# Attention tail: the last 64 queries of both heads of a pair handled as one tile of 128 rows

## The chip, the cores and the metric

The kernel runs on one core of a Trainium2 chip. The metric is the device time of one execution in microseconds. Before the change three runs gave 1061.9, 1064.76 and 1065.36 us, a median of 1064.76 us. The execution that the profiler took is a run of its own.

Engines are named as in the profile: PE is TensorE (PEld is its weight load), DVE is VectorE, ACT is ScalarE, POOL is GpSimd, and SP issues the DMAs.

## What is computed

The reference is three layers, one after the other. Only the first is touched:

```python
B, H, S, D = 2, 8, 576, 64
scores = matmul(q, k.T) / sqrt(D)                # per head, 576 x 576
scores = where(key > query, -1e9, scores)        # causal
a = exp(scores - max); a /= a.sum(-1) + 1e-9
local = a @ v
q_p = where(q > 0, q, exp(q) - 1) + 1
mem = (q_p @ M_prev) / (q_p . z_prev + 1e-6)
x = g * mem + (1 - g) * local                    # g = sigmoid(beta), per head
```

Its output, 1152 tokens by 512, goes through a softplus layer (512 to 2048 to 512) and then through a layer of 8 experts (512 to 1024 to 512 each) whose shares come from 8 rounds of row and column normalization.

## The kernel before, in words

Everything is one launch. The order of all instructions is worked out before by a planner (`Plan`): each operation is added with an engine, an assumed duration, the buffers that it reads and writes and a rank; `Plan.run` then starts, on each engine, the operation of lowest rank that is ready and whose buffers are free, and emits the instructions in the order of these planned starts. On the chip every engine works through its list in that order, and waits where an input is late. Durations are assumed by the small helpers `act`, `dve`, `gps`, `pe`, `dma`; `gps` is for GpSimd. An operation marked as using the shared port is not planned beside another such operation.

Attention runs over 8 units (2 batches, 4 pairs of heads), and in each unit over 5 query tiles, `QT`: four of 128 queries and a tail of 64 (queries 512 to 575). `prep` loads keys and queries of one head (transposed, doubled over the two halves of the partitions) and splits them into rounded parts and remainders in `st` (keys, queries, remainder of queries); `prep_v` loads values, a column of ones, and the queries for the memory branch, whose `phi` it works out.

`softmax(u, i)` computes the scores of one tile for both heads (lines 517 and 518: two products per head and part), adds the mask and takes the row minimum of the scaled negative on DVE (525), exponentiates on ACT (540), transposes the result in blocks of 128 keys on PE (548, 550) into the one PSUM bank `tp`, and copies it to SBUF as `pt` (270, the copy helper). The tail has 576 keys, more than one bank of PSUM holds, so its scores come in two parts of 288, and its rows are 64: one 64-row tile for each head, each with two score parts, one exponential, five transposes and two copies.

`output(u, i, pts)` multiplies `phi` with the memory (568), each head's `pt` with its values, in blocks of 128 keys and 65 columns (575), adds the small constants to the divisors (590), inverts them (592), scales (593), adds memory and local parts on GpSimd (275, the pair helper), transposes both heads at once (596), and `piece` copies the result and its remainder into the inputs of the next layer (270, 610). The output of a tile is ranked two tiles behind its softmax (`AHEAD`). A floating-point product that isn't rounded shows in the trace as two instructions, a transpose as one.

PSUM in attention: two banks `sp` for scores, one `tp`, two `pm`, one `xp`, and two more (`bank`) that scores may use in the first four units. From the fifth unit on the latter go to products of the next layer (676 to 678), which PE runs between those of attention as soon as batch 0 is done.

Of the kernel before, what the change touches and what calls it, by code (L numbers as in the profile page):

```python
# [19 lines left out]
P = 128  # L20
# [34 lines left out]
NPR, NPT = 6, 4  # L55
PS = (2, 1, 2, 1)
QT = [(0, 128), (128, 128), (256, 128), (384, 128), (512, 64)]

# [183 lines left out]
def fused_kernel(ctx, tc, kq, vq, gm, w_in, w_out, wg, w1, w2, out1, out2):  # L242
# [19 lines left out]
    def gps(n, fn, r, w, x=0, **kw):  # L262
        return pl.add("POOL", 90 + 2.23 * n + x, fn, r, w, port=True, **kw)
# [119 lines left out]
    def attention():  # L383
# [12 lines left out]
        mask = pl.buf("ac", [P, 512 + P], F32, "mask")  # L396
        eps = pl.buf("ac", [P, NPAIR, 4], F32, "eps")

# [7 lines left out]
        def consts():  # L406
            def masks():
                nc.gpsimd.memset(mask.ap, 0.0)
                nc.gpsimd.affine_select(
                    out=mask[:, 512:], in_=mask[:, 512:], compare_op=ALU.is_ge, fill=NEG,  # L410
                    base=0, pattern=[[-1, P]], channel_multiplier=1,
                )
                nc.gpsimd.memset(eps[:, :, 0:2], 1e-9)
                nc.gpsimd.memset(eps[:, :, 2:4], 1e-6)

            pl.add("POOL", 2000, masks, [], [mask, eps])

# [34 lines left out]
        def stack(u, j):  # L452
            st = pl.buf("ld", [P, 3, S], F32R, "st", "st")
            U[u]["qs", j] = st
            return st


        def prep(u, j):
            b, p = units[u]
            st = stack(u, j)  # L460
            kqd = pl.buf("ld", [P, 2, S], F32, "kqd", "kqd")
            low = "POOL" if u else "DVE"

            def part(lo, hi):
                n, c, k = hi - lo, slice(lo, hi), ("c", lo)
# [12 lines left out]
        def prep_v(u):  # L478
            b, p = units[u]
            vt = pl.buf("a2", [P, 5 * 130 + S], F32, "vt", "vt")  # L480
            ph = pl.buf("a2", [P, S], F32, "phi", "phi")
            dma(614, lambda: nc.sync.dma_start(vt.ap, vq[b, p]), [vt], late=2000)

            act(S, lambda: nc.scalar.activation(ph.ap, vt[:, 650:], AF.Exp), [vt], [ph])
            dve(S, lambda: nc.vector.tensor_scalar(
                out=ph.ap, in0=ph.ap, scalar1=1.0, scalar2=None, op0=ALU.min), [], [ph], fast=True)
            dve(S, lambda: nc.vector.scalar_tensor_tensor(
# [10 lines left out]
        def softmax(u, i):  # L498
# [3 lines left out]
            if kx <= 512:  # L502
                parts = [(0, max(kx, 256), kx)]
            else:
                parts = [(0, kx // 2, kx // 2), (kx // 2, kx // 2, kx // 2)]
# [5 lines left out]
            def part(k, k0, n, w):  # L511
# [3 lines left out]
                def mm():  # L515
                    for sp, st in zip(sps, sts):
                        nc.tensor.matmul(sp[:R, :n], st[:, 1, q0:kx], st[:, 0, k0:k0 + n], start=True, stop=False)  # L517
                        nc.tensor.matmul(sp[:R, :n], st[:, 2, q0:kx], st[:, 0, k0:k0 + n], start=False, stop=True)  # L518
# [3 lines left out]
                m0 = 512 - q0 + k0  # L522
# [13 lines left out]
            nb = (kx + P - 1) // P  # L536
            nf = min(nb, 4)

            def head(pr, mn):
# [3 lines left out]
                pt = pl.buf("a3", [P, 4 * P + 64], F32, "pt", "pt")  # L543
                tp = pl.buf("psa", [P, 512], F32, "tp", "tp")

                def tr():
                    for t in range(nf):
                        nc.tensor.transpose(tp[:, t * R:(t + 1) * R], pr[:R, t * P:(t + 1) * P], ident[:R, :R])  # L548
                    if nb == 5:
                        nc.tensor.transpose(tp[:64, 4 * R:5 * R], pr[:R, 512:576], ident[:R, :R])  # L550
# [3 lines left out]
                if nb == 5:  # L554
                    copy(R, lambda: pt[:64, 4 * R:5 * R], lambda: tp[:64, 4 * R:5 * R], [tp], [(pt, ("p", 1))],
                         psum=True)
# [3 lines left out]

        def output(u, i, pts):
            b, p = units[u]
# [8 lines left out]
            def pv(j):  # L571
# [7 lines left out]
                pe(nb * (223 if R == P else 119), mm, [pts[j], (vt, ("v", j))], [pm])  # L579
# [66 lines left out]
        return [gms, mask, eps] + [b for (p, t), q in pl.queues.items() if p in apools or p == "psa" for b in q]  # L646
# [798 lines left out]
def _layout(q, k, v, M_prev, z_prev, beta, moe_w_in, moe_w_out, moe2_w_gate, moe2_w1, moe2_w2):  # L1445
# [11 lines left out]
    kq = np.stack([k.transpose(0, 1, 3, 2), q.transpose(0, 1, 3, 2)], 3)  # L1457
# [5 lines left out]
    vq = np.concatenate([vp, q.transpose(0, 1, 3, 2).reshape(B, NPAIR, P, S)], 3)  # L1463
# [31 lines left out]
```

## Time and profile before

| | us |
|---|---|
| median of 3 runs | 1064.76 |
| the profiled execution | 1059.33 |
| its span, first to last instruction | 1057.6 |
| PE busy | 1041.1 (98%) |
| DVE busy | 922.8 (87%) |
| ACT busy | 593.2 (56%) |
| POOL busy | 364.2 (34%) |

Busy time of PE is of matmuls that overlap, with modelled ends. So the time that a group of them takes is read from its start to the start of the next group, not from its busy time. An attention unit is about 20 us of the first 160; the two other layers take the rest.

### The profile page before, as it was taken

Reading aid. Unit: us, or ns where it says so; the run is one execution under the profiler, and the core shown is the slowest. Engines: PE = TensorE matmul, PEld = TensorE weight load, DVE = VectorE, ACT = ScalarE, POOL = GpSimd, SP = SyncE. Lnnn points to the kernel's source line nnn. Section 1 sums busy time; section 2 is a strip of 40 time slices with the busy share of each in tenths; the row PEclk is TensorE's granted clock in tenths of the full one; section 3 lists DMA queues with packets and bytes.
Section 4 is the critical chain, followed back from the end, with each engine's and each line's share of the span. In section 5 each row is a group of like instructions: output and inputs, shape, how many; then the busy total and the mean of one; then the engine's idle time right before and its main releaser. Section 6 shows DMA issues by size and latency. Waiting matters only on the chain.

```text
span 1057.6 us, 14920 instructions
## 1 busy us (share of the span) xinstructions
PE 1041.1 (98%) x5262; PEld 869.7 (82%) x5262; DVE 922.8 (87%) x1738; ACT 593.2 (56%) x1144; POOL 364.2 (34%) x394
## 2 busy tenths in 40 slices
PE   6999999999999999999999999999999999999998
PEld 5888888788887878888888888888888888888886
DVE  6777779787868699999999999999999999999977
ACT  5787675656374766355554555545555455554542
POOL 3565535131342332434234233332333323233220
PEclk9999899999999999999999999999999999999999
DMA  5543111333320111211211111110121111111002
GB/s 203 172 141 112 64 62 40 100 100 100 99 81 21 60 41 48 84 41 59 76 45 60 53 48 60 60 60 29 53 79 42 60 45 56 56 54 59 22 20 90
DMA packets 28558, 72.89 MB, mean 69 GB/s; under 512 B 2684, under 2 KB 11972, under 8 KB 28484
## 3 DMA queue, kind: packets, MB, share of 16 engines
q1 hardware_dynamic: 28484, 71.95, 21.1%
q8 instruction: 41, 0.67, 0.3%
q14 instruction: 33, 0.27, 0.1%
HBM read 69.54 MB, written 2.40 MB: 68 GB/s over the span
## 4 chain that ended last, share of the span: by engine, by line
PE 93%; DVE 4%; ACT 1%; issue 1%; DMA 0%; POOL 0%; SPq 0%; DVEq 0%; ACTq 0%; POOLq 0%
PE pa L1185 6%; PE dA L1359 6%; PE pa L1186 6%; PE dA L1361 6%; PE pa L1187 6%; PE dA L1360 5%; PE pm L575 4%; PE pc L1185 3%; PE pc L1187 3%; PE pc L1186 3%; PE dC L1361 3%; PE dC L1360 3%; PE dC L1359 3%; PE tp L548 2%; PE dn L828 2%; PE dn L826 2%
## 5 line engine op out<-in xcount | busy, mean ns | idle before, releaser
L275 POOL TENSOR_TENSOR ws<-raw 128x256 f32<-128x256 f32 x128 | 124.7, 975 | 440.7 <-issue 20.4
L270 ACT ACTIVATE fh<-u 128x512 fp32r<-128x512 f32 x160 | 99.9, 627 | 100.8 <-DVE u L1285 51.8
L276 DVE TENSOR_TENSOR fl<-u,fh 128x512 fp32r<-128x512 f32 x160 | 115.7, 724 | 7.3 <-ACT fh L270 7.3
L1236 ACT ACTIVATE u<-pa 128x512 f32<-128x512 f32 x64 | 38.0, 594 | 64.8 <-PE pa L1187 64.1
L1376 DVE TENSOR_TENSOR acc<-dA,acc 128x512 f32<-128x512 f32 x92 | 61.7, 683 | 5.5 <-PE dA L1361 5.3
L270 ACT ACTIVATE fh<-t 128x512 fp32r<-128x512 f32 x64 | 38.6, 623 | 41.4 <-DVE t L1285 41.4
L575 PE MATMUL pm<-vt,pt 128*128 128x65 f32 (+2 forms) x480 | 58.5, 260 | 0.0
L575 PEld LDWEIGHTS pm<-vt,pt 128*128 128x128 f32 (+2 forms) x480 | 53.2, 177 | 4.5 <-issue 1.4
L275 POOL TENSOR_TENSOR ws<-raw,ws 128x256 f32<-128x256 f32 x64 | 55.1, 861 | 0.0
L275 POOL TENSOR_TENSOR ws<-ws,raw 128x256 f32<-128x256 f32 x64 | 53.0, 829 | 4.9
L270 ACT ACTIVATE pt<-tp 128x256 f32<-128x256 f32 (+3 forms) x96 | 35.4, 386 | 26.3 <-PE tp L548 17.5
L540 ACT ACTIVATE pr<-pr,mn 128x128 f32<-128x128 f32 (+4 forms) x80 | 45.6, 599 | 6.3 <-DVE mn L525 5.9
L1240 DVE TENSOR_TENSOR u<-pc,u 128x512 f32<-128x512 f32 x64 | 43.7, 683 | 3.5 <-PE pc L1187 1.8
L1256 ACT ACTIVATE pb<-pa 128x512 f32<-128x512 f32 x32 | 18.6, 582 | 48.9 <-PE pa L1187 44.8
L525 DVE CUSTOM_DVE_ANT_0 pr<-sp,mask 128x128 f32<-128x128 f32 (+4 forms) x80 | 36.3, 473 | 9.6 <-PE sp L518 4.5
L276 DVE TENSOR_TENSOR fl<-t,fh 128x512 fp32r<-128x512 f32 x64 | 44.1, 689 | 0.0
L275 POOL TENSOR_TENSOR st<-kqd,st 64x576 fp32r<-64x576 f32 (+1 forms) x28 | 40.3, 1444 | 8.0 <-DVE st L271 3.2
L1249 DVE SCALAR_TENSOR_TENSOR u<-u,pb 128x512 f32<-128x512 f32 x56 | 41.8, 746 | 0.6
L1376 DVE TENSOR_TENSOR acc<-dC,acc 128x512 f32<-128x512 f32 x62 | 40.9, 681 | 0.1
L517 PE MATMUL sp<-st 128*128 128x256 f32 (+3 forms) x96 | 34.8, 374 | 5.5 <-DVE st L276 5.5
L548 PE MATMUL tp<-ident,pr 128*128 128x128 f32 (+1 forms) x224 | 37.6, 273 | 2.7 <-ACT pt L270 2.1
L275 POOL TENSOR_TENSOR gl<-u,gh 128x512 fp32r<-128x512 f32 x12 | 15.5, 1296 | 62.0 <-ACT u L753 61.5
(5121 smaller groups left out, 3607.5 us busy)
## 6 DMA issues: line engine op xcount, KB each, us to landing
raw<-w SPq DMA_DIRECT2D x64, 512.0 KB, 3.5
raw<-w_in SPq DMA_DIRECT2D x16, 512.0 KB, 3.5
raw<-w_out SPq DMA_DIRECT2D x16, 512.0 KB, 3.5
kqd<-kq SPq DMA_DIRECT2D x14, 576.0 KB, 3.7
vt<-vq SPq DMA_DIRECT2D x8, 613.0 KB, 5.3
pb<-gates SPq DMA_DIRECT2D x16, 256.0 KB, 5.3
out<-acc SPq DMA_DIRECT2D x9, 256.0 KB, 2.0
kqd<-kq SPq DMA_DIRECT2D x2, 320.0 KB, 4.3
```

Of the source, the lines that this page charges most:

```text
L270: return act(n, lambda: nc.scalar.activation(out(), src(), AF.Copy), r, w, x=-42 if psum else 0, **kw)
L275: return gps(n, lambda: nc.gpsimd.tensor_tensor(out=out(), in0=a(), in1=b(), op=op), r, w, **kw)
L276: return dve(n, lambda: nc.vector.tensor_tensor(out=out(), in0=a(), in1=b(), op=op), r, w, port=True, **kw)
L548: nc.tensor.transpose(tp[:, t * R:(t + 1) * R], pr[:R, t * P:(t + 1) * P], ident[:R, :R])
L575: nc.tensor.matmul(pm[:R, j * 65:(j + 1) * 65], pts[j][:kk, t * R:(t + 1) * R], vt[:kk, t * 130 + j * 65:t * 130 + (j + 1) * 65], start=(t ...
L1185: nc.tensor.matmul(o[:, :CH], wh[:, at], h(), start=start and k == 0, stop=False, **kw)
L1186: nc.tensor.matmul(o[:, :CH], wh[:, at], l(), start=False, stop=False, **kw)
L1187: nc.tensor.matmul(o[:, :CH], wl[:, at], h(), start=False, stop=(k == 1), **kw)
L1359: nc.tensor.matmul(o[:, :CH], wh[:, at], h.ap, start=start and n == 0, stop=False, **kw)
L1360: nc.tensor.matmul(o[:, :CH], wh[:, at], l.ap, start=False, stop=False, **kw)
L1361: nc.tensor.matmul(o[:, :CH], wl[:, at], h.ap, start=False, stop=(n == 1), **kw)
L1376: dve(CH, lambda: nc.vector.tensor_tensor(out=acc[c][:, cs_], in0=o[:, :CH], in1=acc[c][:, cs_], op=ALU.add), [o], [a_])
```

## The change

The query columns of each head are laid out on the host with 128 columns in the tail, in which head 0 fills the first 64 and head 1 the last 64, and the rest is zero. The queries of the memory branch get a second copy of their last 64 columns. So the products of both heads can be accumulated into one score tile of 128 rows. The tail has one softmax (`both`) and one output (`output2`) for both heads. Rows 0 to 63 of the product with the values are used from the columns of head 0, rows 64 to 127 from those of head 1; the scaled rows are written into the two diagonal blocks of a tile `z`, zero elsewhere, and a product of `z` with two stacked identities (`fold`) replaces the transpose. Masks and these constants are made by more GpSimd operations at the start. `pr` has 5 buffers in place of 6. GpSimd's assumed duration in the planner goes from 90 + 2.23 n to 160 + 2.2 n ns.

```diff
-NPR, NPT = 6, 4
+NPR, NPT = 5, 4
 PS = (2, 1, 2, 1)
 QT = [(0, 128), (128, 128), (256, 128), (384, 128), (512, 64)]
+SQ = S + D
+TAIL = len(QT) - 1
...
-        return pl.add("POOL", 90 + 2.23 * n + x, fn, r, w, port=True, **kw)
+        return pl.add("POOL", 160 + 2.2 * n + x, fn, r, w, port=True, **kw)
...
-        mask = pl.buf("ac", [P, 512 + P], F32, "mask")
+        mask = pl.buf("ac", [P, 512], F32, "mask")
         eps = pl.buf("ac", [P, NPAIR, 4], F32, "eps")
+        mask2 = pl.buf("ac", [P, S // 2], F32, "mask2")
+        fold = pl.buf("ac", [P, D], F32, "fold")
+        z = pl.buf("ac", [P, P], F32, "z")
...
+            def tails():
+                nc.gpsimd.memset(mask2.ap, 0.0)
+                for j in range(2):
+                    r = slice(j * D, (j + 1) * D)
+                    nc.gpsimd.affine_select(
+                        out=mask2[r, :], in_=mask2[r, :], compare_op=ALU.is_ge, fill=NEG,
+                        base=512 - S // 2, pattern=[[-1, S // 2]], channel_multiplier=1,
+                    )
+                    nc.gpsimd.tensor_copy(fold[r, :], ident[r, r])
+                nc.gpsimd.memset(z.ap, 0.0)
...
-                dma(n, lambda: nc.sync.dma_start(kqd[:, :, c], kq[b, 2 * p + j, :, :, c]), [(kqd, k)],
-                    late=2500 if lo or u else 0)
-                kd, w = [(kqd, k)], [(st, k)]
-                copy(n, lambda: st[:, 0, c], lambda: kqd[:, 0, c], kd, w, eng="DVE")
-                copy(n, lambda: st[:, 1, c], lambda: kqd[:, 1, c], kd, w)
-                pair(n, lambda: st[D:, 0, c], lambda: kqd[D:, 0, c], lambda: st[D:, 0, c].bitcast(F32),
+                qhi = SQ if hi == S else hi
+                n, m, k = hi - lo, qhi - lo, ("c", lo)
+                kc, qc = slice(lo, hi), slice(S + lo, S + qhi)
+                lc = slice(S + SQ + lo, S + SQ + qhi)
+                src, late = kq[b, 2 * p + j], 2500 if lo or u else 0
+                if n == S:
+                    dma(608, lambda: nc.sync.dma_start(kqd.ap, src), [kqd], late=late)
+                elif not lo:
+                    def two(x):
+                        return x[:, :2 * S].rearrange("p (a c) -> p a c", a=2)[:, :, :hi]
+                    dma(n, lambda: nc.sync.dma_start(two(kqd), two(src)), [(kqd, ("c", 0, 0))], late=late)
+                else:
+                    for r, c in enumerate((kc, qc)):
+                        dma((c.stop - c.start) // 2, lambda c=c: nc.sync.dma_start(kqd[:, c], src[:, c]),
+                            [(kqd, ("c", lo, r))], late=late)
+                kd, w = [(kqd, ("c", lo, r)) for r in range(2 if lo else 1)], [(st, k)]
+                if n == S:
+                    kd = [kqd]
+                copy(n, lambda: st[:, kc], lambda: kqd[:, kc], kd, w, eng="DVE")
+                copy(m, lambda: st[:, qc], lambda: kqd[:, qc], kd, w)
+                pair(n, lambda: st[D:, kc], lambda: kqd[D:, kc], lambda: st[D:, kc].bitcast(F32),
                      ALU.subtract, kd, w, eng=low)
-                pair(n, lambda: st[:, 2, c], lambda: kqd[:, 1, c], lambda: st[:, 1, c].bitcast(F32),
+                pair(m, lambda: st[:, lc], lambda: kqd[:, qc], lambda: st[:, qc].bitcast(F32),
                      ALU.subtract, kd, w, eng=low)
...
+            dma(646, lambda: nc.sync.dma_start(vt.ap, vq[b, p]), [vt], late=2000)
...
+            if i == TAIL:
+                return both(u, sts)
+            parts = [(0, max(kx, 256), kx)]
...
-                pe(nb * (R / 1.2 + (3 if R == P else 9)), tr, [pr], [tp])
-                copy(nf * R, lambda: pt[:, :nf * R], lambda: tp[:, :nf * R], [tp], [(pt, ("p", 0))], psum=True)
-                if nb == 5:
-                    copy(R, lambda: pt[:64, 4 * R:5 * R], lambda: tp[:64, 4 * R:5 * R], [tp], [(pt, ("p", 1))],
-                         psum=True)
...
+        def both(u, sts):
+            w = S // 2
+            pr = pl.buf("a3", [P, S], F32, "pr", "pr")
+            mn = pl.buf("sm", [P, 2], F32, "mn", "mn")
+            def part(k):
+                k0 = k * w
+                sp = bank("sp") if not k and u < NPAIR else pl.buf("psa", [P, 512], F32, "sp", "sp")
+                def mm():
+                    for n, st in enumerate(sts):
+                        for m in range(2):
+                            q = S + m * SQ + 512
+                            nc.tensor.matmul(sp[:, :w], st[:, q:q + P], st[:, k0:k0 + w],
+                                             start=(n + m == 0), stop=(n + m == 2))
+                pe(4 * mms(w) + 30, mm, sts, [sp])
+                dve(w, lambda: nc.vector.tensor_tensor_reduce(
+                    out=pr[:, k0:k0 + w], in0=sp[:, :w], in1=mask2.ap if k else mask[:, :w], op0=ALU.add, op1=ALU.min, scale=-0.125,
+                    scalar=mn[:, 0:1] if k else 3.0e38, accum_out=mn[:, k:k + 1]),
+                    [sp, mask if not k else mask2], [pr, mn])
+                return sp
+            part(0)
+            sp = part(1)
+            act(S, lambda: nc.scalar.activation(pr.ap, pr.ap, AF.Exp, bias=mn[:, 1:2], scale=-1.0), [mn], [pr], x=93)
+            pt = pl.buf("a3", [P, 5 * P], F32, "pt", "pt")
+            tp = pl.buf("psa", [P, 512], F32, "tp", "tp")
+            def tr():
+                for t in range(4):
+                    nc.tensor.transpose(tp[:, t * P:(t + 1) * P], pr[:, t * P:(t + 1) * P], ident)
+            pe(4 * 110, tr, [pr], [tp])
+            pe(110, lambda: nc.tensor.transpose(sp[:D, 384:512], pr[:, 512:S], ident), [pr], [sp])
+            copy(512, lambda: pt[:, :512], lambda: tp.ap, [tp], [(pt, ("p", 0))], psum=True)
+            copy(P, lambda: pt[:D, 512:], lambda: sp[:D, 384:512], [sp], [(pt, ("p", 1))], psum=True)
+            return pt
+        def output2(u, pt):
+            b, p = units[u]
+            vt, ph = U[u]["v"], U[u]["phi"]
+            pm = pl.buf("psa", [P, 512], F32, "pm", "pm")
+            pe(220, lambda: nc.tensor.matmul(pm[:, 130:260], ph[:, 512:SQ], mds(u), start=True, stop=True),
+               [ph, (gms, ("g", b))], [pm])
+            def mm():
+                for t in range(5):
+                    kk = min(P, S - t * P)
+                    nc.tensor.matmul(pm[:, :130], pt[:kk, t * P:(t + 1) * P], vt[:kk, t * 130:(t + 1) * 130],
+                                     start=(t == 0), stop=(t == 4))
+            pe(5 * 225 + 80, mm, [pt, vt], [pm])
+            l = pl.buf("sm", [P, 4, 1], F32, "l", "l")
+            x = pl.buf("a3", [P, 4, D], F32, "x", "x")
+            xp = pl.buf("psa", [P, 512], F32, "xp", "xp")
+            def own(j):
+                r = slice(j * D, (j + 1) * D)
+                return r, pm[r, 0:260].rearrange("r (a j c) -> r a j c", a=2, j=2)[:, :, j]
+            def divisors(j):
+                def fn():
+                    r, v = own(j)
+                    nc.vector.tensor_tensor(
+                        out=l[r, 0:2], in0=v[:, :, 64:65], in1=eps[r, p, j::2].unsqueeze(2), op=ALU.add)
+                dve(2, fn, [pm, eps], [(l, ("j", j))])
+            def scaled(j):
+                def fn():
+                    r, v = own(j)
+                    nc.vector.tensor_tensor(out=x[r, 0:2], in0=v[:, :, 0:64], in1=l[r, 0:2].to_broadcast([D, 2, D]),
+                                            op=ALU.mult)
+                dve(128, fn, [pm, l], [(x, ("j", j))])
+                r = slice(j * D, (j + 1) * D)
+                pair(D, lambda: z[r, r], lambda: x[r, 0], lambda: x[r, 1], ALU.add, [(x, ("j", j))], [(z, ("j", j))])
+            for j in range(2):
+                divisors(j)
+            dve(10, lambda: nc.vector.reciprocal(out=l[:, 0:2], in_=l[:, 0:2]), [], [l])
+            for j in range(2):
+                scaled(j)
+            last = pe(220, lambda: nc.tensor.matmul(xp[:, :D], z.ap, fold.ap, start=True, stop=True), [z, fold], [xp])
+            t0 = b * S + 512
+            c = max(k for k in range(NCH) if CO[k] <= t0)
+            piece(c, p, t0 - CO[c], D, xp, 0)
+            return last
...
+    kq = np.zeros((B, H, D, S + SQ), np.float32)
+    kq[..., :S] = k.transpose(0, 1, 3, 2)
+    kq[..., S:S + 512] = qt[..., :512]
+    for j in range(2):
+        kq[:, j::2, :, S + 512 + j * D:S + 512 + (j + 1) * D] = qt[:, j::2, :, 512:]
```

## Rows read from the trace of the kernel before

**Rows 1.** Chain of waits that ended last, from the page.

```profile
PE 93%; DVE 4%; ACT 1%; issue 1%; DMA 0%; POOL 0%; SPq 0%; DVEq 0%; ACTq 0%; POOLq 0%
```

**Rows 2.** Engines by stretch; columns: stretch, length, busy us (instructions), granted clock, DMA.

```profile
40.00:60.00 20.00, 19.74 (x161) 17.21 (x159) 13.05 (x57) 16.27 (x42) 11.83 (x13) 1.00 0.36 119
...
100.00:120.00 20.00, 19.18 (x138) 16.71 (x137) 12.80 (x52) 14.99 (x37) 9.77 (x10) 0.88 0.11 32
120.00:140.00 20.00, 20.00 (x153) 17.78 (x154) 15.09 (x63) 13.38 (x38) 7.28 (x9) 0.95 0.25 86
...
160.00:1057.60 897.60, 892.35 (x4166) 742.19 (x4164) 807.93 (x1301) 475.67 (x851) 285.05 (x300) 1.00 0.19 59
```

**Rows 3.** PE in order of time around tails: start us, busy us, operation, times.

```profile
129.14 0.38 PE L517 MATMUL sp<-st 128*64 128x288 f32 x1
...
129.75 0.60 PE L548 MATMUL tp<-ident,pr 128*128 128x128 f32 x4
130.19 0.39 PE L568 MATMUL pm<-gms,phi 128*128 128x130 f32 x2
130.41 1.90 PE L575 MATMUL pm<-vt,pt 128*128 128x65 f32 x16
132.24 0.46 PE L548 MATMUL tp<-ident,pr 64*128 64x64 f32 x4
...
132.69 0.39 PE L517 MATMUL sp<-st 128*128 128x256 f32 x1
...
133.47 0.44 PE L568 MATMUL pm<-gms,phi 128*64 128x130 f32 x2
133.83 0.46 PE L548 MATMUL tp<-ident,pr 64*128 64x64 f32 x4
...
134.28 0.94 PE L575 MATMUL pm<-vt,pt 128*64 128x65 f32 x10
135.15 0.33 PE L596 MATMUL xp<-ident,x 128*128 128x128 f32 x1
...
138.70 0.27 PE L596 MATMUL xp<-ident,x 64*128 64x64 f32 x1
138.91 0.49 PE L568 MATMUL pm<-gms,phi 128*128 128x130 f32 x2
```

**Rows 4.** PE in order of time, 112 to 118 us, same columns.

```profile
113.62 0.33 PE L596 MATMUL xp<-ident,x 128*128 128x128 f32 x1 [0.82 <-POOL x L275]
...
116.56 1.48 PE L575 MATMUL pm<-vt,pt 128*64 128x65 f32 x10
117.97 0.47 PE L548 MATMUL tp<-ident,pr 128*128 128x128 f32 x1
```

**Rows 5.** PE in order of time, from one tile's scores to the next.

```profile
107.80 0.38 PE L517 MATMUL sp<-st 128*64 128x288 f32 x1
...
110.80 0.36 PE L517 MATMUL sp<-st 128*128 128x256 f32 x1
```

**Rows 6.** ScalarE groups by shape, 0 to 165 us: count | busy us, mean ns | idle.

```profile
L540 ACT ACTIVATE pr<-pr,mn 64x576 f32<-64x576 f32 x16 | 11.9, 768 | 0.6 <-DVE mn L525 0.6
```

**Rows 7.** VectorE groups by shape, same stretch and columns.

```profile
L525 DVE CUSTOM_DVE_ANT_0 pr<-sp,mask,mn 64x288 f32<-64x288 f32 x16 | 7.5, 503 | 0.0
...
L593 DVE TENSOR_TENSOR x<-pm,l 64x256 f32<-64x256 f32 x8 | 3.3, 411 | 0.3
```

**Rows 8.** GpSimd groups by shape, same stretch and columns.

```profile
L275 POOL TENSOR_TENSOR st<-kqd,st 128x576 fp32r<-128x576 f32 x14 | 19.7, 1409 | 0.7 <-ACT st L270 0.6
L275 POOL TENSOR_TENSOR x<-x 128x128 f32<-128x128 f32 x32 | 16.9, 531 | 29.0 <-DVE x L593 20.7 <-PE sp L518 3.7 <-PE tp L548 2.0
...
L408 POOL MEMSET mask<- 128x640 f32 x1 | 0.6, 634 | 0.0
```

**Rows 9.** SP's queue in order of time: start, issue us, transfers.

```profile
3.96 0.60 SPq L482 DMA_DIRECT2D vt<-vq  x1
```

**Rows 10.** GpSimd in order of time, after its first constants.

```profile
11.09 0.21 POOL L445 TENSOR_TENSOR gms<-gms 128x8 f32<-128x8 f32 x1 [8.61 <-DMA gms<-gm]
```

More of the change, by code (lines that the diff above doesn't have):

```diff
@@ L409, in masks @@
                 nc.gpsimd.affine_select(
-                    out=mask[:, 512:], in_=mask[:, 512:], compare_op=ALU.is_ge, fill=NEG,
+                    out=mask[:, 384:], in_=mask[:, 384:], compare_op=ALU.is_ge, fill=NEG,
                     base=0, pattern=[[-1, P]], channel_multiplier=1,
@@ L414, in masks @@
                 nc.gpsimd.memset(eps[:, :, 2:4], 1e-6)
+            def tails():
[8 more added lines that the diff above has]
+                nc.gpsimd.memset(z.ap, 0.0)
             pl.add("POOL", 2000, masks, [], [mask, eps])
+            pl.add("POOL", 3000, tails, [], [mask2, fold, z])
         NM = B * NPAIR * 130
@@ L501, in softmax @@
             sts = [U[u]["qs", j] for j in range(2)]
[L502 to L505, printed above, removed]
+            if i == TAIL:
+                return both(u, sts)
+            parts = [(0, max(kx, 256), kx)]
+            qh, ql = slice(S + q0, S + q0 + R), slice(S + SQ + q0, S + SQ + q0 + R)
             prs = [pl.buf("a3", [P, S], F32, "pr", "pr") for j in range(2)]
@@ L535, in softmax @@
             k = len(parts)
-            nb = (kx + P - 1) // P
-            nf = min(nb, 4)
+            nb = kx // P
             def head(pr, mn):
@@ L552, in head @@
-                pe(nb * (R / 1.2 + (3 if R == P else 9)), tr, [pr], [tp])
-                copy(nf * R, lambda: pt[:, :nf * R], lambda: tp[:, :nf * R], [tp], [(pt, ("p", 0))], psum=True)
-                if nb == 5:
-                    copy(R, lambda: pt[:64, 4 * R:5 * R], lambda: tp[:64, 4 * R:5 * R], [tp], [(pt, ("p", 1))],
-                         psum=True)
+                    for t in range(nb):
+                        nc.tensor.transpose(tp[:, t * P:(t + 1) * P], pr[:, t * P:(t + 1) * P], ident)
@@ L557, in head @@
+                pe(nb * 110, tr, [pr], [tp])
+                copy(nb * P, lambda: pt[:, :nb * P], lambda: tp[:, :nb * P], [tp], [pt], psum=True)
                 return pt
             return [head(pr, mn) for pr, mn in zip(prs, mns)]
+        def both(u, sts):
[20 more added lines that the diff above has]
+            act(S, lambda: nc.scalar.activation(pr.ap, pr.ap, AF.Exp, bias=mn[:, 1:2], scale=-1.0), [mn], [pr], x=93)
+            pt = pl.buf("a3", [P, 5 * P], F32, "pt", "pt")
+            tp = pl.buf("psa", [P, 512], F32, "tp", "tp")
+            def tr():
+                for t in range(4):
+                    nc.tensor.transpose(tp[:, t * P:(t + 1) * P], pr[:, t * P:(t + 1) * P], ident)
+            pe(4 * 110, tr, [pr], [tp])
[3 more added lines that the diff above has]
+            return pt
@@ L561, in output @@
         def output(u, i, pts):
+            if i == TAIL:
+                return output2(u, pts)
             b, p = units[u]
@@ L645, in attention @@
             output(*todo.pop(0))
-        return [gms, mask, eps] + [b for (p, t), q in pl.queues.items() if p in apools or p == "psa" for b in q]
+        return [gms, mask, eps, mask2, fold, z] + [b for (p, t), q in pl.queues.items() if p in apools or p == "psa" for b in q]
     def turned(src, name):
@@ L1456, in _layout @@
     gm[:, n:] = np.concatenate([bt, bt], 1).reshape(-1)
-    kq = np.stack([k.transpose(0, 1, 3, 2), q.transpose(0, 1, 3, 2)], 3)
+    qt = q.transpose(0, 1, 3, 2)
+    kq = np.zeros((B, H, D, S + SQ), np.float32)
[3 more added lines that the diff above has]
+        kq[:, j::2, :, S + 512 + j * D:S + 512 + (j + 1) * D] = qt[:, j::2, :, 512:]
     kq = np.concatenate([kq, kq], 2)
@@ L1462, in _layout @@
     vp = vp.reshape(B, NPAIR, 5, P, 130).transpose(0, 1, 3, 2, 4).reshape(B, NPAIR, P, 650)
-    vq = np.concatenate([vp, q.transpose(0, 1, 3, 2).reshape(B, NPAIR, P, S)], 3)
+    qt = qt.reshape(B, NPAIR, P, S)
+    vq = np.concatenate([vp, qt, qt[..., 512:]], 3)
     return {
```

28 lines of the change are left out of this document (11 added, 17 removed).

## The prediction

> **What bounds the kernel now.** I read three views, in this order. First the chain of waits that ended last: PE holds 93% of it and no other engine more than 4% [rows 1]. Second the engines by stretch, because a share over the whole span mixes attention with the two layers behind it. In attention PE is busy 19.2 to 20.0 us of each 20, while ACT has 13.4 to 16.3, DVE 12.8 to 15.1 and POOL 7.3 to 11.8; behind attention it is busy 892.35 us of 897.6 [rows 2]. So PE bounds both parts, and what comes off PE's list in attention shifts all that follows by as much. Third PE in order of time around the tails, since busy times of overlapped matmuls overstate: I take the distance from the start of one group to the start of the next [rows 3]. The reader is to see there that PE goes from group to group without an idle mark, and that narrow groups (64 queries) cost nearly as much as wide ones.
>
> **The change on PE, per unit.** All distances are from [rows 3].
> Transposes: each head's five narrow ones take 132.24 to 132.69, 0.45 us, so 0.90 for two heads. Afterwards there are four wide ones, 129.75 to 130.19, 0.44, and one more of 0.11: 0.55. Saved 0.35.
> Values: each head's ten narrow instructions (five products, two instructions each) take 134.28 to 135.15, 0.87, so 1.74. Afterwards there are ten wide ones with both heads' 130 columns. The trace has no such run. The cheap end is the wide run of 65 columns: 16 in 130.41 to 132.24, 1.83, or 0.114 each, hence 1.14. A pair with 130 columns, the memory product, takes 130.19 to 130.41, 0.22, which says the same (0.11 each). The dear end is that a wide instruction costs twice a narrow one, 0.174, hence 1.74 and nothing saved. I take the near rows, both of 128 wide: saved 0.60.
> Memory product: narrow 133.47 to 133.83, 0.36; wide 0.22. Saved 0.14. The narrow one may hold a wait, so 0 is the lower end.
> Last step: the narrow transpose 138.70 to 138.91, 0.21, becomes a product of two instructions, 2 x 0.114 = 0.23. Lost 0.02.
> Scores: eight instructions of 288 columns before, 129.14 to 129.75 for a part of four, 0.61; eight of 288 columns afterwards. Padding makes their weights wide; four wide ones of 256 columns start 132.69 and are over before 133.47, so width is not the price there. Zero.
> Sum 0.35 + 0.60 + 0.14 - 0.02 = 1.07 us per unit, over 8 units 8.6 us. By the ends, 0.35 - 0.02 = 0.33 or 2.6 us below; above, if half of each narrow group's 0.36 for two instructions is a cost of changing shapes, some 0.15 more for each of the two heads, 11 us.
>
> A rule of the Trainium skill speaks against the largest term. On the row, a narrow instruction of the value product costs 0.87 / 10 = 0.087 and a wide one 0.114, a ratio of 0.76 [rows 3]. "TensorE: Matmul & The Clock Gate", section "LDWEIGHTS (loading the stationary operand)", says that loading weights takes a time in proportion to their columns and not to their rows. By that rule a 64-column load is half of a 128-column one, twenty narrow ones cost what ten wide ones do, and the value product saves nothing. The trace agrees in direction and not in size; I go by the row, and the rule's case is the second rival.
>
> **Beside PE.** ACT: one exponential fewer per unit, 0.768 us [rows 6]; copies out of PSUM fall from four to two. DVE: one mask operation of each of the two parts fewer, about 2 x 0.5 us; one addition and one scaling more, less than 0.411 each [rows 7]. So both get lighter in the sum, and neither can take PE's place. POOL: the remainder of the queries is 640 columns wide in place of 576, 1.409 x 64 / 576 = 0.16 us twice per unit, and the one addition of the tail becomes two, each between 0.21 (the 8-column operation [rows 10]) and 0.53 (128 columns [rows 8]). That is at most 0.9 us per 20 us on an engine that has 8 us free: hidden. If that cover goes, PE waits for the tail's addition as it did for another tile's at 113.62, 0.82 us [rows 4].
>
> Start: the second piece of keys and queries goes in two transfers per head in place of one, so everything behind them on SP's queue, the values and the memory too, is issued two issues later, 2 x 0.60 = 1.2 us [rows 9]. The memory's landing is what POOL waited for at 11.09 [rows 10]. Between nothing (other work is there) and 1.2 us; I take 0.2, since PE still works on the first scores and transposes then. The new masks and constants on POOL: the memset of 640 columns took 0.634 [rows 8]; five operations on at most 288 columns and a few of 64 are under 3.5 us even at that price each, and POOL then idles until 11.09 with 8.61 us to spare [rows 10]. Zero.
>
> Longer assumed GpSimd times: the planner counted 90 + 2.23 x 128 = 375 ns for an addition that takes 531, and will count 442; for 576 columns 1374, then 1427, with 1409 measured [rows 8]. The order of all later work may move. Behind attention PE has 897.6 - 892.35 = 5.2 us without work [rows 2], which is the most that a better order can give; a worse one has no such end. I take zero.
>
> An added hold: the fifth transpose goes into the bank of the second score part, which so stays taken through mask operation, exponential, transposes and copies. From the fifth unit on the next tile's scores for both heads need both `sp` banks, so they queue behind that at four hand-overs (after units 4, 5, 6 and 7 of 8). Now the next tile's scores start 110.80 - 107.80 = 3.0 us after the second part's [rows 5]. The hold is about 0.6 (scores) + 0.5 (mask) + 0.77 (exponential) + 0.55 (transposes) + two copies of at most 0.77 = 4.0 us, so up to 1.0 late, 4.0 us in all; nothing at the other end, as PE has outputs of earlier tiles and products of the next layer to run. I take 0.8 us for all four.
>
> **Sum.** -8.6 + 0.2 + 0.8 = -7.6 us. Against the profiled execution, 1059.33 (span 1057.6), that is 1051.7. The median of the runs, 1064.76, lies 5.4 above it, and nothing in the profile says which of its parts would differ, so I take the same difference from the median: **1057.2 us**.
>
> **The rivals.**
> *Slower: the tail's single chain runs PE dry, and its clock falls.* One score tile, one exponential and one `tp` use for both heads leave nothing to alternate with, and at the four hand-overs the held bank stops PE. In 100 to 140 us the granted clock was 0.88 and 0.95 of full [rows 2]: 0.12 x 20 / 0.5 + 0.05 x 20 / 0.5 = 6.8 us at 1.2 in place of 2.4 GHz, at most 3.4 us lost; a value product took 116.56 to 117.97, 1.41, in place of 0.87, and an idle stretch of 0.82 lay ahead [rows 4]. If each hand-over brings a wait of 1.0 and such a fall, 4 x 4.4 = 17.6 against the 8.6 saved and the 0.2 lost: 1064.8 + 9.2 = 1074. It decides from two such falls on. Against it: POOL, ACT and DVE get lighter, and products of the next layer are there to fill. Chance 0.07.
> *The wide value product costs twice a narrow one.* What is left is 0.35 + 0.14 - 0.02 = 0.47 per unit, 3.8 us, less 1.0: 1062.0. For it: the dear end above. Against it: two wide rows at 0.11. Chance 0.14.
> *The fall of the clock at 115 us goes.* The 0.82 us before it were a wait for GpSimd [rows 4], whose operations the planner now sees longer, and narrow transposes and products, which become fewer. Then 3.4 more are saved: 1053.8. No row here tells the two apart. Against it: the fall may have another place in another run. Chance 0.20.
> *Other engines' chains bound the unit.* If GpSimd's additions or the longer output chain of the tail (two additions, two scalings, two GpSimd operations in place of one each) hold PE 0.5 us in each unit, half the gain goes: 1061. For it: the wait of 0.82; against: the output is ranked two tiles behind. Chance 0.11.
>
> **How the numbers follow.** The forecast itself has 0.48; its own range is 1054 to 1060. The range for 8 in 10 goes down to the case without the fall with some of the upper end of the PE sum, 1050, and up to the case of a dear value product with a microsecond or two of holds, 1063.5. About 0.3% (3.2 us) is what a measurement can tell: faster means below 1061.6. The forecast nearly always (0.46), the clock case (0.20), and four in ten of the second and the fourth rival (0.10) are there: 0.76. Slower needs above 1068: most of the first rival, 0.06. The rest, 0.18, is the same.
>
> **What would show it.** Right: per unit one group of four wide transposes and one of about 0.11; ten value instructions of 130 columns in 1.1 to 1.2 us; the first wide expert product some 7 to 9 us earlier, and a distance between the two programs that stays as it is from there to the end. Wrong: a value group near 1.7 us; idle marks of PE before the first scores of units 5 to 8, put down to the copy of the fifth transpose; granted clock under 1.00 at several tails; PE busy behind attention less close to its span than 892.35 of 897.6.

## The result, and the profile after

| | us |
|---|---|
| changed kernel, 6 runs | 1045.77 to 1048.41, median 1047.01 |
| kernel before, 6 runs | 1056.53 to 1065.75, median 1063.33 |
| ratio, 95% interval | 0.986, 0.9823 to 0.9897 |
| profiled execution (its span), before | 1059.33 (1057.6) |
| profiled execution (its span), after | 1047.08 (1045.2) |

The change gained 16.3 us by the medians and 12.3 between the two profiled executions; 7.6 were forecast, and 1047.0 lies under the range. The kernel before spreads over 9 us, the changed one over 3. The changed kernel has the same bound, PE, by its chain of waits:

```profile
PE 90%; ACT 4%; DVE 4%; issue 1%; POOL 1%; DMA 0%; SPq 0%; DVEq 0%; ACTq 0%; POOLq 0%
```

The engines by stretch of the changed kernel, the columns of [rows 2] (busy time of PE, PE's weight load, DVE, ACT and POOL, in this order):

```profile
40.00:60.00 20.00, 19.83 (x157) 18.35 (x156) 14.17 (x62) 15.22 (x39) 14.28 (x17) 1.00 0.50 161
100.00:120.00 20.00, 19.41 (x150) 17.83 (x149) 16.66 (x60) 15.56 (x40) 10.64 (x12) 1.00 0.24 86
120.00:140.00 20.00, 20.00 (x159) 18.46 (x158) 15.86 (x63) 14.20 (x37) 8.43 (x13) 1.00 0.17 55
...
160.00:1045.20 885.20, 880.87 (x4108) 731.74 (x4106) 799.78 (x1287) 464.06 (x840) 289.63 (x296) 1.00 0.19 59
```

The granted clock is 1.00 where it was 0.88 and 0.95 [rows 2]. Behind 160 us PE has 885.2 - 880.87 = 4.3 us without work, before 5.2. The gain is in attention: the first product with the second layer's output weights (`dn`) starts 12.7 us earlier, the first expert product (`pa`) 12.0 (7 to 9 forecast), and at the end the spans differ by 12.4. Kernel before, then changed kernel:

```profile
169.70 0.39 PE L826 MATMUL dn<-gh,wo0h 128*128 128x512 f32 x1
338.06 0.50 PE L1185 MATMUL pa<-xh,a000h 128*128 128x512 f32 x1
```

```profile
157.04 0.39 PE L944 MATMUL dn<-gh,wo0h 128*128 128x512 f32 x1
326.08 0.50 PE L1303 MATMUL pa<-xh,a000h 128*128 128x512 f32 x1
```

The tail of the changed kernel on PE in order of time, the columns of [rows 3]:

```profile
127.92 0.33 PE L671 MATMUL xp<-fold,z 128*128 128x64 f32 x2
128.06 0.48 PE L549 MATMUL sp<-st 128*128 128x512 f32 x1
...
132.16 0.78 PE L600 MATMUL sp<-st 128*128 128x288 f32 x4
132.78 0.60 PE L579 MATMUL tp<-ident,pr 128*128 128x128 f32 x4
...
135.46 0.27 PE L621 MATMUL sp<-ident,pr 128*64 128x128 f32 x1
135.57 0.62 PE L618 MATMUL tp<-ident,pr 128*128 128x128 f32 x4
136.03 1.00 PE L693 MATMUL pm<-vt,pt 128*128 128x65 f32 x8
137.02 0.33 PE L714 MATMUL xp<-ident,x 128*128 128x128 f32 x1
137.18 0.39 PE L630 MATMUL pm<-gms,phi 128*128 128x130 f32 x2
137.41 1.48 PE L636 MATMUL pm<-vt,pt 128*128 128x130 f32 x10
138.81 0.50 PE L794 MATMUL ph<-xh,wi2h 128*128 128x512 f32 x1
```

From start to start, as in the prediction: transposes 135.46 to 136.03, 0.57 (forecast 0.55); value product 137.41 to 138.81, 1.40 (1.14); memory product 0.23 (0.22); last step 127.92 to 128.06, 0.14 (0.23); a part of the scores 0.62 (0.61). The value product takes 1.40 or 1.41 us in all 8 units. Together 2.34 us where the same groups took 0.90 + 1.74 + 0.36 + 0.21 = 3.21 before [rows 3]: 0.87 per unit in place of 1.07, 7.0 us over 8 units in place of 8.6.

So by these groups the forecast's own sum is nearly there, and the rest is somewhere else. PE's waits from 15 to 130 us (engine and line, whom it waited for: us in total, times, longest) are, of the kernel before:

```profile
PE xp L596 <- DVE l L592: 2.2, 1, 2.2
PE xp L596 <- POOL x L275: 0.8, 1, 0.8
PE tp L548 <- ACT pt L270: 0.8, 2, 0.5
```

and of the changed kernel:

```profile
PE tp L579 <- ACT pt L272: 1.7, 4, 0.6
PE xp L714 <- DVE l L708: 0.8, 1, 0.8
PE xp L714 <- POOL x L277: 0.6, 1, 0.6
```

The single wait of 2.2 us is gone, and the others have grown from 1.6 to 3.1 in sum. Waits alone explain 0.7 us of what is missing. The fall of the clock in the profiled execution before is at most 3.4 us more, which leaves over 1 us of the 12.3 without a place.

### The profile page after: what moved, and what is told of

The parts are those of the page before. It is cut to its first block, busy times and chain, and to the rows that moved or that the text cites. A ratio compares the mean times of both kernels' runs of the same rounds, so it can differ in the third digit from the quotient of the medians.

```text
span 1045.2 us, 14608 instructions
## 1 busy us (share of the span) xinstructions
PE 1030.2 (99%) x5150; PEld 865.8 (83%) x5150; DVE 925.8 (89%) x1722; ACT 584.6 (56%) x1122; POOL 378.1 (36%) x408
## 4 chain that ended last, share of the span: by engine, by line
PE 90%; ACT 4%; DVE 4%; issue 1%; POOL 1%; DMA 0%; SPq 0%; DVEq 0%; ACTq 0%; POOLq 0%
PE pa L1303 6%; PE pa L1304 6%; PE pa L1305 6%; PE dA L1478 5%; PE dA L1477 5%; PE dA L1479 5%; PE pc L1305 3%; PE pc L1303 3%; PE pc L1304 3%; PE dC L1478 3%; PE dC L1477 3%; PE dC L1479 3%; PE dn L945 2%; PE dn L946 2%; PE dn L944 2%; PE pm L693 2%
## 5 line engine op out<-in xcount | busy, mean ns | idle before, releaser
L278 DVE TENSOR_TENSOR fl<-u,fh 128x512 fp32r<-128x512 f32 x160 | 112.3, 703 | 1.9 <-ACT fh L272 1.8
L277 POOL TENSOR_TENSOR ws<-raw,ws 128x256 f32<-128x256 f32 x64 | 60.9, 952 | 0.0
L277 POOL TENSOR_TENSOR ws<-ws,raw 128x256 f32<-128x256 f32 x64 | 58.4, 913 | 4.9
L693 PE MATMUL pm<-vt,pt 128*128 128x65 f32 x320 | 42.1, 268 | 0.0
L272 ACT ACTIVATE pt<-tp 128x512 f32<-128x512 f32 (+3 forms) x72 | 32.6, 452 | 15.0 <-PE tp L579 11.9
L693 PEld LDWEIGHTS pm<-vt,pt 128*128 128x128 f32 x320 | 40.6, 194 | 0.0
L571 ACT ACTIVATE pr<-pr,mn 128x128 f32<-128x128 f32 (+3 forms) x64 | 34.1, 561 | 8.2 <-DVE mn L557 7.6
L579 PE MATMUL tp<-ident,pr 128*128 128x128 f32 x160 | 30.0, 286 | 3.6 <-ACT pt L272 3.0
L557 DVE CUSTOM_DVE_ANT_0 pr<-sp,mask 128x128 f32<-128x128 f32 (+3 forms) x64 | 29.4, 485 | 2.1 <-PE sp L550 1.4
L549 PE MATMUL sp<-st 128*128 128x256 f32 (+2 forms) x64 | 24.4, 391 | 5.2 <-DVE st L278 5.2
```

The source lines that it names most:

```text
L272: return act(n, lambda: nc.scalar.activation(out(), src(), AF.Copy), r, w, x=-42 if psum else 0, **kw)
L277: return gps(n, lambda: nc.gpsimd.tensor_tensor(out=out(), in0=a(), in1=b(), op=op), r, w, **kw)
L278: return dve(n, lambda: nc.vector.tensor_tensor(out=out(), in0=a(), in1=b(), op=op), r, w, port=True, **kw)
L693: nc.tensor.matmul(pm[:R, j * 65:(j + 1) * 65], pts[j][:kk, t * R:(t + 1) * R], vt[:kk, t * 130 + j * 65:t * 130 + (j + 1) * 65], start=(t ...
```

## The experiments

The granted clock of each run is the mean over its execution, its end included (0.99 in the last 17.6 us of the profiled kernel before). A fall is a stretch at 1.2 in place of 2.4 GHz. Kernels measured together share the runs of the kernel before.

Two theories stood at the start. A: the clock of the kernel before falls with the narrow work of its tails. B: it falls behind waits for GpSimd, which the planner does not foresee because it assumes GpSimd's operations to be too short.

**The kernel before once more, run by run.** No edit.

> The kernel before once more, for its granted clock run by run. Theories A and B: its times spread from 1056 to 1066, and the granted clock goes with them: 0.997 or more at 1056 to 1059 and about 0.992 at 1065, since 9 us more are 18 us of 1057 at half the clock. Theory C (the spread is something else, transfers for instance): the clock is the same, about 0.997, at 1056 and at 1065.

Its 12 runs, and 29 of the same kernel measured later, in groups by granted clock:

| clock | 12 runs | 29 runs |
|---|---|---|
| 1.000 | 1 at 1057.0 | 3 at 1056.5 to 1056.7 |
| 0.996, 0.997 | 3 at 1059.0 to 1059.2 | 2 at 1058.7 to 1059.0 |
| 0.993 to 0.995 | 2 at 1061.7 to 1061.8 | 7 at 1061.6 to 1062.1 |
| 0.990 to 0.992 | 6 at 1064.3 to 1066.1 | 17 at 1064.0 to 1065.7 |

Time goes with the clock, so theory C falls. Without a fall the kernel before takes 1056.5; its median holds 7 us of falls, the profile that I had read only 3 (6.8 us at 1.2 GHz). Of 53 more runs four are at 1.000, at 1056.4 to 1056.7. The changed kernel is never under 0.998.

**GpSimd's old times in the changed kernel; its new ones in the kernel before.**

```diff
-        return pl.add("POOL", 160 + 2.2 * n + x, fn, r, w, port=True, **kw)
+        return pl.add("POOL", 90 + 2.23 * n + x, fn, r, w, port=True, **kw)
```

> The changed kernel with GpSimd's old assumed times (90 + 2.23 n), so the merged tail alone. Theory A: 1046 to 1049 in all runs, clock 0.998 or more, as the changed kernel. Theory B: some runs 3 to 9 us longer at a clock under 0.997, 1046 to 1058.

Six runs, 1048.1 to 1050.9, clock 0.998 or more; ratio to before 0.9888, 0.9868 to 0.9909. The merged tail alone brings 8.4 us between runs at full clock (1056.5 to 1048.1), and without the new times too no run is under 0.998. PE waits three times for the tail's longer output chain (`z`), 2.6 us in sum, where the changed kernel has no such wait; the longest is at 142.9 us (same columns):

```profile
PE xp L671 <- POOL z L277: 1.8, 1, 1.8
```

So here is the fourth rival's mechanism, three times and 2.6 us long in all; the new times remove it, and the runs at full clock go from 1048.1 to 1045.8 to 1046.9.

```diff
-        return pl.add("POOL", 90 + 2.23 * n + x, fn, r, w, port=True, **kw)
+        return pl.add("POOL", 160 + 2.23 * n + x, fn, r, w, port=True, **kw)
```

With the changed kernel's own 2.2 in place of 2.23 the planned order of the kernel before deadlocks, so there is no time for it.

> The kernel before with GpSimd's longer assumed times alone (160 + 2.23 n; a coefficient next to the changed kernel's). Theory A (the clock falls with the narrow work of the tails): falls stay, times spread over 1055 to 1066 with clocks from 0.990 to 1.000, median 1059 or more. Theory B (the falls follow waits that the planner misses for GpSimd's sake): all runs at 1054 to 1058, clock 0.998 or more.

Median 1056.74 (ratio 0.9956, 0.9935 to 0.9976): 7 of 12 runs at 1.000 and 1055.9 to 1056.9, five at 0.995 to 0.998 and 1059.5 to 1062.3. Without a fall it is as fast as before; it just falls more seldom. Both theories miss: narrow tails are there and falls get rare (against A), yet they don't vanish (against B). At 21.7 us its trace has a wait of 0.6 us in place of 2.2:

```profile
22.33 0.66 PE L548 MATMUL tp<-ident,pr 128*128 128x128 f32 x4 [0.60 <-ACT pt L270]
```

**Tails of 128 queries for each head, nothing merged.**

```diff
-QT = [(0, 128), (128, 128), (256, 128), (384, 128), (512, 64)]
+QT = [(0, 128), (128, 128), (256, 128), (384, 128), (448, 128)]
...
+                if nb == 5:
+                    pe(110, lambda: nc.tensor.transpose(sp[:64, 384:512], pr[:, 512:576], ident), [pr], [sp])
```

> The kernel before, but the tail of each head is a tile of 128 queries (448 to 575, of which 64 are worked out twice), nothing merged; the fifth transpose goes to the score bank. More work and no narrow matmuls: per unit 0.2 us more for transposes, 0.5 for the value product, 0.2 less for the memory product and the last transpose, about 0.5, so 4 us in all over the runs of before that have no fall (1056.5). Theory A: all runs at 1058 to 1062 with a clock of 0.998 or more, under the median of before. Theory B: spread as before, 1060 to 1071, with clocks under 0.997.

Median 1057.07 (ratio 0.9967, 0.9949 to 0.9985), nine of 12 runs at 1056.3 to 1057.7, three at 0.997 and 1060.6 to 1060.9. Hardly any narrow work (the fifth block alone), and still falls: A fails again. The 4 us more did not come either: the runs at 0.999 or more lie within 1 us of before's. Its profiled execution has its fall after the 2 us wait that it shares with the kernel before, here its waits and its stretch of 20 to 40 us, with 0.17 x 20 / 0.5 = 6.8 us at 1.2 GHz:

```profile
PE xp L597 <- DVE l L593: 2.0, 1, 2.0
```

```profile
20.00:40.00 20.00, 17.99 (x124) 17.30 (x123) 12.35 (x48) 12.55 (x34) 10.57 (x11) 0.83 0.36 116
```

**Wide products added to the narrow tails.**

```diff
+                    if R < P:
+                        for _ in range(2):
+                            nc.tensor.matmul(pm[:, 260:512], sts[j][:, 0, :P], sts[j][:, 0, :252], start=True,
+                                             stop=True, skip_group_check=True)
```

> The kernel before, with two products of 128 wide weights and 252 columns added behind each head's narrow value product of a tail (results unused), 32 in all, 0.11 to 0.2 us each with the change of shape, so 3.5 to 6.5 us more work than before's runs without a fall (1056.5). Theory A: the added wide work keeps the clock up, 0.998 or more in most runs, 1060 to 1063 and hardly any spread; if order or waits make the falls, the spread stays and the times lie at 1060 to 1072 with clocks down to 0.990.

Median 1062.57, 1059.7 to 1065.4: three runs at 0.999 or more, nine at 0.994 to 0.996. Added wide work does not keep the clock up; its profile too has a wait of 2.0 us, at 22.7 us, and a fall behind it, 0.26 x 20 / 0.5 = 10.4 us at 1.2 GHz:

```profile
20.00:40.00 20.00, 17.96 (x115) 16.08 (x114) 11.08 (x41) 10.85 (x28) 7.59 (x8) 0.74 0.22 74
```

This is the third result against A.

**Only scores, mask and exponential merged.** Transposes, value and memory product and output stay per head and narrow.

```diff
+                    for t in range(4):
+                        nc.tensor.transpose(tp[:, t * D:(t + 1) * D], pr[r, t * P:(t + 1) * P], ident[r, r])
...
-            if i == TAIL:
-                return output2(u, pts)
```

> The changed kernel, but only scores, mask and exponential of the tail are merged; transposes, value products, memory product and output are per head and narrow as before. Theory A: TensorE's list is as long as before's (the scores take 0.61 us per part in both), so the runs without a fall lie at 1054 to 1057, and falls stay: median 1058 or more. Theory D (the gain comes from the lighter ScalarE and VectorE): 1046 to 1051.

1060.0 to 1062.0 in all 12 runs at 0.998 or more, in neither of the ranges expected. Of the gain of the changed kernel nothing is left, although ScalarE has one exponential per unit less: theory D falls. That the gain is in the narrow groups on PE fits this, but does not follow from it alone, since its order also waits more. From 15 to 175 us PE waits 7.0 us, in the kernel before 3.8; that is most of the 3.5 us by which it is slower than before without falls. The longest wait lies behind attention, at 168 us, and 160 to 180 us has a granted clock of 0.91:

```profile
PE pot L778 <- ACT po L272: 2.4, 1, 2.4
```

**One or two transposes put later in the kernel before.** By now the suspect was not the narrow work but two waits: theory E. Only the order of the kernel before is changed, after planning.

```diff
+MOVES = {1: 2, 27: 1}
...
+        for k, n in MOVES.items():
+            i = line.index(turns[k])
+            if n > 0:
+                behind(turns[k], line[i + n])
```

`turns` are the outputs' last PE operations, counted from 0, `line` is PE's order, and `behind` puts an operation, and what follows from it, behind another: `1: 2` puts operation 1 of `turns` two places later. The first two kernels have one of the entries each, the third has both.

> The kernel before, with one PE operation put two places later in the order: the transpose at the end of tile 1 of the first unit, for which PE stood still 2.2 us at 21.7 us; what only follows from it is put behind it. Nothing else is changed. Theory E: the clock of the kernel before falls at two places, after this wait (some 10 us at 1.2 GHz, 5 us lost) and after the wait of 0.8 us at 112.8 (6.8 us, 3 us lost), each in some of its runs. Then this kernel shows 1056 (clock 1.000) and 1059 (0.997) and nothing above 1060.5. If the falls do not follow these waits, it spreads as before, up to 1065 and down to 0.990.

Eight runs: five at 1.000 (1055.3 to 1056.4), three at 0.997 (1057.6 to 1058.4), nothing below. As E said. Its profiled execution, at 1.000, still has the wait of 0.8 us at 112.8 us, and no fall behind it.

> The kernel before, with the transpose for which PE stood still 0.8 us at 112.8 us put one place later (behind the next value product). Theory E: the fall at 115 us is gone, the one at 25 us stays: 1056 (1.000) and 1061.7 (0.993 to 0.995), nothing at 1059 and nothing above 1063. Otherwise as before, up to 1066.

Twelve runs: four at 1.000 (1055.5 to 1055.8), four at 0.997 (1057.9 to 1058.3), four at 0.995 (1060.2 to 1061.1). Nothing at 0.993 or below. The two lower groups, which I had not expected, fit a fall of two lengths at the first wait; only an execution at 0.995 was profiled. It shows the wait (PE in order of time), and the stretch with 0.26 x 20 / 0.5 = 10.4 us at 1.2 GHz, while 100 to 120 us are now at 1.00:

```profile
22.10 0.44 PE L587 MATMUL pm<-gms,phi 128*128 128x130 f32 x2
24.76 0.45 PE L615 MATMUL xp<-ident,x 128*128 128x128 f32 x1 [2.22 <-DVE l L611]
```

```profile
20.00:40.00 20.00, 17.78 (x112) 15.58 (x110) 11.71 (x45) 11.37 (x30) 10.04 (x10) 0.74 0.31 103
100.00:120.00 20.00, 20.00 (x154) 17.13 (x153) 14.55 (x60) 17.07 (x45) 8.55 (x10) 1.00 0.19 62
```

> The kernel before, with both transposes put later. Theory E: no fall in any run, 1055 to 1057 with a clock of 0.998 or more, so 6 to 7 us under the median of before for about 2 us of removed waiting. Otherwise as before, 1056 to 1066 with clocks down to 0.990.

Six runs, 1054.0 to 1055.4, all at 0.999 or more; median 1055.01 against 1064.18 of the kernel before, measured with it, ratio 0.993, 0.9906 to 0.9954. The narrow tails are all still there. Two transposes put later win 9 us. Their waits were 3.0 us, of which 1.1 comes back as a wait for a copy, at 21.8 us, in these six runs without a fall:

```profile
PE tp L567 <- ACT pt L289: 1.9, 3, 1.1
```

**A wait put into the changed kernel.** A first try put two operations of PE behind the last step of tile 2 (`MOVES = {2: -2}`).

> The changed kernel, with a wait put in: the two PE operations ahead of the last step of tile 2 of the first unit (the memory product and the value product of the merged tail) go behind it, so PE stands still there at about 24.5 us, 1 to 1.5 us long, until VectorE and GpSimd have worked out its input. Theory E: 1 us more in every run and a fall of the clock in some, 1047 to 1049 at 0.998 or more, and 1050 to 1053 at 0.993 to 0.997. If a wait alone does not bring a fall, all runs lie at 1047 to 1049 with 0.998 or more.

1047.0 to 1049.3 in six runs. It tells nothing of the wait that it was to bring: PE has no wait marked there. But its profiled execution, at 0.998, has a fall of 0.09 x 20 / 0.5 = 3.6 us behind a wait that the changed kernel has too, at 69.7 us; the changed kernel's profiled execution has none there. So the merged kernel isn't free of falls; they are rarer or shorter.

```profile
70.52 0.37 PE L734 MATMUL xp<-ident,x 128*128 128x128 f32 x1 [0.78 <-DVE l L728]
```

```profile
60.00:80.00 20.00, 18.17 (x130) 16.74 (x129) 16.81 (x58) 15.35 (x38) 9.77 (x11) 0.91 0.51 173
```

The second kernel works out useless sums on GpSimd ahead of one addition:

```diff
+                if (u, i) == (0, 1):
+                    for _ in range(6):
+                        nc.gpsimd.tensor_tensor(out=z.ap, in0=z.ap, in1=z.ap, op=ALU.add)
```

> The changed kernel, with six additions of a zero tile to itself (128 x 128, about 0.5 us each) ahead of the addition of tile 1 of the first unit on GpSimd, and the planner not told. PE stands still at the last step of that tile, at about 21.4 us, for up to 2 to 3 us. Theory E: in part of the runs the clock falls after it for 6.8 to 10 us, so runs fall apart in two groups, some 3 to 5 us from each other: 1048 to 1050 at 0.999 or more and 1051 to 1055 at 0.995 to 0.997. If the narrow tails of before are needed for a fall, one group, 1047 to 1050, none under 0.998.

Five runs at 1049.1 to 1049.5 and 0.999 or more, one at 1053.8 and 0.994. The wait, in its trace:

```profile
20.41 0.27 PE L621 MATMUL sp<-ident,pr 128*64 128x128 f32 x1
22.76 0.33 PE L720 MATMUL xp<-ident,x 128*128 128x128 f32 x1 [2.08 <-POOL x L717]
```

So 2.1 us of waiting cost about 2 us in every run, and one of six lost 4.4 more at a lower clock; that run was not profiled, so the place of its fall is not shown. Narrow tails are not needed for a fall. Why one in six here and most runs in the kernel before is open.

**Small steps beyond the changed kernel.** The fifth block of keys 128 high, its values padded with zeros:

```diff
-            pe(110, lambda: nc.tensor.transpose(sp[:D, 384:512], pr[:, 512:S], ident), [pr], [sp])
+            pe(110, lambda: nc.tensor.transpose(sp[:, 384:512], pr[:, S - P:S], ident), [pr], [sp])
```

> The changed kernel, but the fifth block of keys is 128 high too (keys 448 to 575, with zeros for the values of the first 64, which the fourth block has already). In the changed kernel the two instructions of the 64 high block take 0.209 us each to the next start, the others 0.112 to 0.124. If the change of height is the price, this saves up to 2 x 0.09 us per unit, 1.4 us in all: 0.9985 of the changed kernel, 1045 to 1046. If height costs nothing by itself (a wait stood there), the time is the same as the changed kernel's, 1046 to 1048.

1045.8 to 1047.1, median 1046.5, ratio to before 0.9846, 0.9821 to 0.9871. PE in order of time shows a value product of 24.74 - 23.62 = 1.12 us in place of 1.40:

```profile
23.62 1.28 PE L635 MATMUL pm<-vt,pt 128*128 128x130 f32 x10
24.74 0.27 PE L713 MATMUL xp<-ident,x 128*128 128x128 f32 x1
```

So the change of height is the price (0.28 per unit). In the profiled execution `dn` starts 2.4 us earlier (154.63 for 157.04), but in time the interval overlaps the changed kernel's, and 2 us are not seen. With two transposes put later as well (`MOVES = {16: 2, 27: 1}`):

> The changed kernel with the fifth block of keys 128 high, and two transposes for which PE stood still 0.77 us at 68 and 0.59 us at 104 us put later in PE's order (behind the next scores and behind the next value product). Theory E: the waits are gone, up to 1.3 us, and with the first of them the falls of 3.4 us at 70 us that runs of the merged kernel still show (clock 0.998, 1.7 us): all runs at 1044.5 to 1046 with 0.999 or more. If the waits only move, 1046 to 1047 as without.

1046.3 to 1047.3, clock 0.999 or more: no gain. Its trace has waits of 0.8 us at 71 and 0.7 at 108.5 us in place of those taken away: they only moved.

## Why the prediction was wrong, step by step

- *PE bounds, and what leaves its list in attention is won*: right. From the kernel before without its two waits (1055.0) to the changed one (1047.0) it is 8.0 us, for 8.6 forecast on PE and 7.6 in all. In their profiled executions `dn` starts at 165.07 and 157.04, 8.0 apart too. The sum is near in part by luck: PE's work from 18 us to there, all distances from start to start without the marked waits, goes from 145.17 to 136.24 us. That is 8.9 less, of which the priced groups hold 7.0, and waits take 1.1 back. The rest lies in groups that I had not priced, such as the next layer's products between them (`ph`, 96 in both kernels), at 23.1 in place of 24.1 us; why is not shown.
- *Transposes, memory product, scores*: within 0.02 us. *Last step*: 0.09 cheaper than forecast. *Value product*: forecast 1.14, measured 1.40, so 0.34 saved in place of 0.60, because I priced the 64 high block as a wide one; made 128 high it takes 1.12. By the rule of the Trainium skill, "TensorE: Matmul & The Clock Gate", section "LDWEIGHTS (loading the stationary operand)", as the prediction works it out, the value product saves nothing. For instructions 128 rows high the trace agrees. The second to the eighth instruction of the narrow group start at 134.39 to 134.74 us, 0.058 us apart (the group's start is 134.28 [rows 3]), those of the wide group after at 137.52 to 138.19, 0.112 apart. The two of the 64 high block behind them take 0.20 to 0.22 us each of the wide group's 1.40. My 0.087 for a narrow instruction was a mean over these and the two of the 64 high block. What is saved is the price of that block, which two heads pay twice and the merged tail once.
- *Hold of the score bank* (0.8 us): no wait of PE for the score banks stands among its waits. *Start* (0.2 us): not seen; PE's first scores start at 5.20 us, before at 5.55.
- *Longer assumed GpSimd times: zero*: wrong in size. In the merged kernel they take away 2.6 us of waits and bring about 2 us between runs at full clock; in the kernel before they bring nothing at full clock and make falls rarer.
- **The step that failed** is "I take the same difference from the median", with the rival "the fall of the clock at 115 us goes" at 3.4 us and a chance of 0.20. I had seen that the profiled execution lies 5.4 us under the median and wrote that nothing says which part would differ. The runs show it: the median holds falls at two places, behind a wait of 2.2 us at 21.7 us and one of 0.8 at 112.8; without either 1055.0 in place of 1064.2. So the 16.3 us are 6.8 of falls (1063.3 to 1056.5), 1.5 of the two waits themselves (to 1055.0) and 8.0 of the rest. The first wait stood as the longest idle time of PE behind the start, and no step of mine touched it: "PE is busy 19.2 to 20.0 us of each 20" was read from 40 us on. The stretch ahead of that in the kernel before, and the wait in it, are

```profile
20.00:40.00 20.00, 17.78 (x149) 16.05 (x148) 15.21 (x60) 14.82 (x38) 11.59 (x12) 1.00 0.36 130
```

```profile
23.88 0.30 PE L596 MATMUL xp<-ident,x 128*128 128x128 f32 x1 [2.22 <-DVE l L592]
```

Both waits are properties of one planned order. A change makes that order anew, and the first wait can go with it (GpSimd times alone: 0.6 us left) or stay (tails of 128 queries, added wide products: 2.0). It does not take the merged tail to lose the falls: the GpSimd times alone make them rare, and two moved instructions end them. Not all of the lost time is placed: with one wait alone the groups of runs lie up to 1.8 us (wait at 112.8) or 4.9 us (at 21.7) apart, while the slowest runs of the kernel before lie 9 above 1056.5.

- *Slower through falls at four hand-overs*: the mechanism (a wait brings a fall) exists, the sign was the other way round: the kernel before had most of the falls.

## What to carry to other kernels

Runs of one kernel that spread more than its measurement does are to be explained before a change to it is priced: here their granted clock gave 1056.5 without falls and a median 7 us above. A stretch left out of a reading can hold the wait that decides. In an order written by a planner, look for PE's single longest waits; they belong to this order, not to the kernel, and moving one instruction behind the next group can be worth more than the work that a change saves. When a group of narrow matmuls is made wide, price the odd block that keeps its shape by itself, since a mean over the group hides it.

## What was not expected of the hardware

- A wait of PE of 0.8 us at 112.8 us was followed by 6.8 us at 1.2 GHz in two profiled executions of the kernel before, and by none in that of the kernel without the first wait. One of 2.0 to 2.2 us that began at 20.7 to 22.8 us was followed by 6.8 us (tails of 128 queries) or 10.4 (added wide products; second wait removed), and by none in two executions of the kernel before and one of the merged kernel with a wait put in. One of 0.8 us at 70 us was followed by 3.6 us in one execution of the merged kernel and by none in others.
- Tails of 128 queries per head, with half of the work done twice, took within 1 us of narrow ones at full clock, though their value products take 1.30 us for each head in place of 0.87. Part of what this should cost is found: PE waits 2.4 us from 15 us on in place of 3.8, and from `dn` to the end it is 886.8 us in place of 887.9.
- Ten wide value instructions of which two have 64 rows take 1.40 us, and 1.12 with all at 128 rows.
